# DeltaNet with a multiplicative feed-forward layer on one core: loads on one queue, clears as steps, a new order of all steps

## The chip, the core and the metric

The kernel runs on one core of a Trainium2 chip. The metric is device time in microseconds (us), the median of several runs. The core has five instruction queues: TensorE (PE, with its weight loads as PEld), VectorE (DVE), ScalarE (ACT), GpSimd (POOL) and SyncE (SP). Each works through its own queue in order and waits on semaphores where it needs a result of another. Loads and stores are issued by one of these queues and carried out by 16 DMA engines.

## The reference

Two stages follow each other. The first is a delta rule over 768 tokens for 4 batches of 8 heads of width 48; the second is a feed-forward layer over the 3072 rows of 384 values that come out of it.

```python
k_n = k / (np.linalg.norm(k, axis=-1, keepdims=True) + 1e-06)
for t in range(S):
    y[:, :, t] = einsum('bhd,bhde->bhe', q[:, :, t], state)
    v_old = einsum('bhde,bhd->bhe', state, k_n[:, :, t])
    state += beta[:, :, t] * outer(k_n[:, :, t], v[:, :, t] - v_old)
x = y.transpose(0, 2, 1, 3).reshape(3072, 384)
a, b = x @ w1, x @ w2                 # 384 x 1024 each
out = ((a * b) @ w3) @ w_out          # 1024 x 1024, 1024 x 384
```

The four weight matrices lie in memory in double precision; the kernel turns them into float32 itself.

## The kernel before

The 768 tokens are cut into 12 chunks of 64, and two chunks form a pair. Within a chunk the delta rule is solved with a triangular inverse; between chunks a state is carried on. The kernel is written as steps of many small parts, each a Python generator, and every `next` of a part issues one step's instructions. The parts, with the letter that names them in the list:

- `k`, `q`, `v`, `p` load K, Q and V; `p` loads K and then Q of a chunk in a second layout, into the buffers `perm` and `spare` (`load_perm`, L246, issues at L253). `k` and `q` use `load_crossed` (L225) and `load_tok` (L236). For chunk 0, `k` and `q` are issued on ScalarE's queue (L1205, L1216), everything else on SyncE's.
- `K`, `Q` (chunks 0 and 1) turn K and Q on TensorE (L352) and copy the result into KQ on ScalarE and VectorE (L362, L364); `d` (other chunks) does it on VectorE out of `perm` and `spare` (L339).
- `g`, `N` are the norms of K (squares on GpSimd L285, sums on VectorE L287, a square root by Newton steps, copies on ScalarE L274 and L276).
- `s` are the scores of a chunk: TensorE (L383, L389), VectorE's product (L395), and for some chunks ScalarE's copy (L407) and GpSimd's mask (L409).
- `u` and `V` are the inverse of a pair of chunks. For the first two pairs the scores are copied into `columns` (L446), transposed on VectorE (L466), the unit matrix is copied from Vb to PSUM by ScalarE (L475), and 31 pairs of VectorE operations follow (L484, L489), which are a chain of their own, with a transpose behind them (L503). Later pairs go through memory (L453, L468, L514).
- `e` is the corner, which completes a chunk's inverse: TT is filled (L549, by ScalarE and GpSimd), VectorE transposes part of it (T, L559), then two groups of products on TensorE (L576) with ScalarE's copies between (L601, L621).
- `c` is the chain from chunk to chunk (TensorE L647, VectorE L678, L687, L707, L709), `y` the outputs (TensorE L746, ScalarE L767).
- `P` is one piece of a weight matrix, 36 in all: a load on SyncE (L791) into one of five `raw` buffers, two operations on ScalarE (L799, L802), a shift on VectorE (L804) and an addition on GpSimd (L806). A buffer can be loaded again when GpSimd has added.
- `t` transposes a piece of w3 on TensorE (L841) and copies it into w3T on ScalarE (L844); `f` folds w3 and w_out into one matrix on TensorE (L855, copied at L862), in two halves for each of eight blocks.
- `a` and `b` compute a * b for the first pair's tokens (L875, L887, L891); `a`, `h`, `i`, `j` do it for later pairs with eleven products in place of more (L994, L1002, L1010, L1031, L1041). `S`, `o`, `x` multiply by the folded matrix and store (L1075, L1104, L1121 to L1166).

`ORDER`, a list of some 1,460 names, says which part takes its next step; each engine then executes its instructions in exactly that order (`in_text_order`, L168). So the list decides what is queued behind what on all five queues.

Buffers that must hold zeros are made by `padded` (L194): it allocates them and clears the whole of them, or all from a column on, on GpSimd (L198) as the program is written down, which puts all clears ahead of the list's steps: TT (2048 values a partition), perm, spare (1024 each), x_room (512), four ktok (16 each), U, T11 (8 each), late (520) and T22 (512). V0's first step, the clear of Vb (L461, L462), stands behind them.

## Time and profile before

| | |
|---|---|
| median of 3 runs | 552.52 us (552.31 to 554.47) |
| profiled execution | 554.45 us |
| its span, first to last instruction | 552.7 us |
| mean granted TensorE clock | 0.994 |
| busy: VectorE, ScalarE, GpSimd | 362.1, 187.6, 253.6 us |
| read from and written to memory by the core | 41.25 and 8.91 MB |

A row of instructions in order of time gives its start, its length, the engine and line, the operation with the tiles it writes and reads, the count, and in brackets how long the engine stood idle before it and what ended that. A row of the chain of work that ended last gives start, length and what it was. "SPq" and "ACTq" are the queues issuing a DMA. Matmuls are pipelined, so the lengths of single ones overlap; a group's length is taken from the chain, in which pieces follow each other.

### The profile page before, as it was taken

Reading aid. Unit: us, or ns where it says so; the run is one execution under the profiler, and the core shown is the slowest. Engines: PE = TensorE matmul, PEld = TensorE weight load, DVE = VectorE, ACT = ScalarE, POOL = GpSimd, SP = SyncE. Lnnn points to the kernel's source line nnn. Section 1 sums busy time; section 2 is a strip of 40 time slices with the busy share of each in tenths; the row PEclk is TensorE's granted clock in tenths of the full one; section 3 lists DMA queues with packets and bytes.
Section 4 is the critical chain, followed back from the end, with each engine's and each line's share of the span. In section 5 each row is a group of like instructions: output and inputs, shape, how many; then the busy total and the mean of one; then the engine's idle time right before and its main releaser. Section 6 shows DMA issues by size and latency. Waiting matters only on the chain.

```text
span 552.7 us, 19818 instructions
## 1 busy us (share of the span) xinstructions
PE 521.4 (94%) x8540; PEld 447.8 (81%) x8540; DVE 362.1 (66%) x814; ACT 187.6 (34%) x393; POOL 253.6 (46%) x278
## 2 busy tenths in 40 slices
PE   3686999999999999999999999999999999999997
PEld 2563666688878988889987889988899888998897
DVE  2757877798767878569967579858587654123332
ACT  4788388955633012422022430123231121300000
POOL 8466555453569960365343255510492212342141
PEclk9997999999999999999999999999999999999999
DMA  8987987669356345454553564253601220020001
GB/s 251 203 223 189 199 188 141 120 159 150 55 90 127 80 106 80 61 101 81 114 98 61 79 121 86 86 83 43 125 16 44 62 51 5 9 66 1 0 1 57
DMA packets 197687, 52.64 MB, mean 95 GB/s; under 512 B 185344, under 2 KB 191488, under 8 KB 197600
## 3 DMA queue, kind: packets, MB, share of 16 engines
q1 hardware_dynamic: 193408, 50.59, 44.6%
q10 hardware_dynamic: 4192, 0.79, 0.9%
q8 instruction: 67, 1.10, 0.8%
q14 instruction: 20, 0.16, 0.1%
HBM read 41.25 MB, written 8.91 MB: 91 GB/s over the span
## 4 chain that ended last, share of the span: by engine, by line
PE 80%; DMA 6%; ACT 5%; DVE 4%; SPq 2%; issue 1%; DVEq 0%; ACTq 0%
PE ps_f L994 33%; PE ps_f L1104 19%; PE ps_f L855 7%; PE ps_w L647 6%; PE ps_f L875 6%; PE ps_w L746 4%; PE ps_w L576 2%; DMA X<-in_q_dram 2%; PE ps_w L383 2%; PE ps_w L389 1%; DMA raw<-in_moe_w_dram 1%; DMA ktok<-in_k_dram 1%; SPq L253 1%; DVE KQ L339 1%; ACT raw L802 1%
## 5 line engine op out<-in xcount | busy, mean ns | idle before, releaser
L1002 DVE TENSOR_TENSOR ab<-ab,ps_f 128x512 f32<-128x512 f32 x80 | 54.5, 682 | 57.3 <-PE ps_f L994 56.8
L1075 POOL TENSOR_TENSOR ab<-ab 128x512 f32<-128x512 f32 (+1 forms) x56 | 61.3, 1116 | 41.8 <-PE ps_f L1104 25.4
L994 PE MATMUL ps_f<-xT,w1s 128*128 128x256 f32 x320 | 78.5, 382 | 0.0
L1041 POOL TENSOR_TENSOR ab<-ab,late 128x512 f32<-128x512 f32 x19 | 24.1, 1271 | 107.0 <-DVE ab L1002 106.3
L994 PEld LDWEIGHTS ps_f<-xT,w1s 128*128 128x128 f32 x320 | 59.9, 190 | 7.9
L1104 PE MATMUL ps_f<-w,ab 128*128 128x192 f32 x376 | 65.5, 328 | 0.0
L1104 PEld LDWEIGHTS ps_f<-w,ab 128*128 128x128 f32 x376 | 61.3, 190 | 1.3 <-issue 0.5
L409 POOL TENSOR_TENSOR PT<-PT,smask 128x512 f32<-128x512 f32 x20 | 25.5, 1277 | 54.9 <-ACT PT L407 54.9
L855 PE MATMUL ps_f<-w2s,w3T 128*128 128x384 f32 x128 | 45.9, 510 | 4.9 <-ACT w3T L844 4.9
L1104 PE MATMUL ps_f<-room,ab 128*128 128x192 f32 x272 | 47.2, 328 | 0.0
L500 DVE TENSOR_TENSOR ps_w<-ps_w,tb 128x31 f32<-128x31 f32 (+15 forms) x124 | 43.3, 349 | 4.2
L767 ACT COPY xT<-ps_w 48x256 f32<-48x256 f32 x96 | 30.4, 365 | 44.8 <-PE ps_w L746 44.3
L1104 PEld LDWEIGHTS ps_f<-room,ab 128*128 128x128 f32 x272 | 44.3, 190 | 0.6 <-issue 0.3
L495 DVE TENSOR_TENSOR tb<-ps_w,Ub 128x31 f32<-128x31 f32 (+15 forms) x124 | 41.9, 338 | 3.6 <-ACT ps_w L475 0.3
L1010 ACT COPY ab<-ps_f 128x512 f32<-128x512 f32 x20 | 11.7, 586 | 95.1 <-PE ps_f L994 95.0
L994 PE MATMUL ps_f<-xT,room 128*128 128x256 f32 x160 | 41.3, 385 | 0.3 <-DVE ab L1002 0.2
L855 PEld LDWEIGHTS ps_f<-w2s,w3T 128*128 128x128 f32 x128 | 24.4, 198 | 20.8 <-issue 6.6
L994 PE MATMUL ps_f<-xT,w2s 128*128 128x256 f32 x160 | 40.1, 381 | 0.0
L994 PE MATMUL ps_f<-x_room,w2s 128*128 128x256 f32 x160 | 38.9, 386 | 0.0
L994 PEld LDWEIGHTS ps_f<-xT,room 128*128 128x128 f32 x160 | 29.5, 190 | 5.5 <-DVE ab L1002 1.1
L994 PEld LDWEIGHTS ps_f<-x_room,w2s 128*128 128x128 f32 x160 | 29.5, 190 | 5.1 <-DVE late L1002 1.0
L994 PEld LDWEIGHTS ps_f<-xT,w2s 128*128 128x128 f32 x160 | 30.1, 190 | 4.0
(143 smaller groups left out, 977.2 us busy)
## 6 DMA issues: line engine op xcount, KB each, us to landing
raw<-in_moe_w_dram SPq DMA_DIRECT2D x16, 512.0 KB, 6.7
vtok<-in_v_dram SPq DMA_DIRECT2D x24, 192.0 KB, 4.4
raw<-in_moe_w_dram SPq DMA_DIRECT2D x24, 192.0 KB, 4.9
out_dram<-osb SPq DMA_DIRECT2D x46, 96.0 KB, 1.7
ktok<-in_k_dram SPq DMA_DIRECT2D x44, 96.0 KB, 3.4
raw<-in_moe_w_out_dram SPq DMA_DIRECT2D x8, 384.0 KB, 4.5
perm<-in_k_dram SPq DMA_DIRECT2D x40, 64.0 KB, 2.8
perm<-in_q_dram SPq DMA_DIRECT2D x32, 64.0 KB, 2.8
```

What stands on the lines that cost most here:

```text
L409: pool.tensor_tensor(out=PT, in0=PT, in1=smask[:].unsqueeze(1).to_broadcast([P, H, C]), op=ALU.mult)
L495: dve.tensor_tensor(out=tv, in0=V[:, 0 : s + 1, s : s + 1].to_broadcast([P, s + 1, n]), in1=U[:, s, s + 1 : BS].unsqueeze(1).to_broadcast( ...
L500: dve.tensor_tensor(out=o, in0=o, in1=tv, op=ALU.subtract)
L647: pe.matmul(out(ps, r, h, z), lhsT=lhs(r, h, z), rhs=rhs(r, h, z), start=True, stop=True,)
L767: act.copy(out=xT[f, p:NP:2, b : b + NR, cc, :].rearrange("p a r t -> p r a t"), in_=pyv[f, z, b : b + NR],)
L855: pe.matmul(ps[:, 0:DM], lhsT=w3Ts[jc, kc // 4][:, kc % 4 * P : kc % 4 * P + P], rhs=wo[:, kc], start=(i == 0), stop=(i == KF - 1),)
L875: pe.matmul(ps[:].rearrange("p b c t -> p b (c t)"), lhsT=w[:, m, js], rhs=x[:, m, :, c0:c1].rearrange("p b c t -> p b (c t)"), start=(m = ...
L994: pe.matmul(acc[name][:, n * i : n * i + n], lhsT=ws[b][:, P * i : P * i + P], rhs=xs[x], start=new and k == 0 and i == 0, stop=k == len(t ...
L1002: dve.tensor_tensor(out=o_, in0=x, in1=acc[name], op=ALU.add)
L1041: eng.tensor_tensor(out=Z1, in0=Z1, in1=late, op=ALU.mult)
L1075: pool.tensor_tensor(out=o_, in0=x_, in1=y_, op=op)
L1104: pe.matmul(ps[b][:, b, :], lhsT=block(u, HF * f + i, z)[:, P * b : P * b + P], rhs=ws_[w][:, i], start=first and i == 0 and (b == 0 or n ...
```

## The change

All loads are issued on SyncE's queue. `padded` no longer clears; it notes what is to be cleared and by which engine, and two new parts clear one noted region a step: `zd` (three on VectorE) and `zp` (nine on GpSimd). On VectorE only that part of TT, perm and spare is cleared which is read as zeros without being written: the first 32 of each 64 columns of TT, the upper 16 of each 32 columns of perm and spare. The list has the same steps as before and these twelve, in a new order throughout. The lines of what stands below `padded` move by 13, and by 15 from the table of parts on.

```diff
 ORDER = """
-V0 P0 k0 beta P18 P13 P0 P18 P0 P0 P11 g0 P13 K0 P18 K0 P11 P18 P10 P13 P13 q0 P3 P3 P11 g0 beta
-beta K0 K0 K0 k1 K1 P10 P11 P12 P3 P12 g0 g0 Q0 P10 g0 g0 g0 g0 g0 P8 Q0 Q0 Q0 K1 K1 K1 Q0 K1 P3
...
+V0 zp P13 beta P12 beta P13 beta P13 k0 P12 P13 P0 P0 k1 K0 t5 g0 P0 g0 g0 P12 K0 K0 K0 P11 P11 K0
+P0 zd P12 zd g0 g0 P10 P18 q0 g0 g0 K1 P10 K1 P8 g0 P10 P11 K1 t5 g0 P9 Q0 q1 K1 K1 P18 P11 P10 P8
+Q0 Q0 Q0 Q0 P3 t2 P18 P8 N0 P9 t2 N0 t3 s0 k2 t3 Q1 P5 P3 P18 P9 P2 s0 P8 zp P3 t4 t0 P3 Q1 s0 g1 zp
+s0 Q1 Q1 Q1 s1 s0 g1 zd P5 s1 P1 t0 P1 s1 P2 P1 P9 g1 s0 t1 P5 P2 s1 P5 P2 s1 p2 P4 s1 d2 g1 P6 P7
+d2 zp t4 u0 u0 s0 u1 t10 u1 P19 u0 u1 V0 V0 t1 V0 V0 P4 P6 P4 V0 P7 V0 P6 P1 V0 f1 f0 P4 P7 k3 V0
...
+    zeros = []
+
+    def padded(name, shape, n, start=0, where=None, eng=pool):
         res = []
         for i in range(n):
             t = persist.tile(shape, FP32, name=f"{name}{i}")
-            pool.memset(t[:, start:] if start else t[:], 0.0)
+            zeros.append((eng, where(t) if where else t[:, start:] if start else t[:]))
             res.append(t)
         return res

+    def zero(part):
+        for eng, t in zeros:
+            if (eng is dve) == part:
+                eng.memset(t, 0.0)
+                yield
+
-    TTx = padded("TT", [P, 2, NR, H, C], 1)[0]
+    TTx = padded("TT", [P, 2, NR, H, C], 1, where=lambda t: t[:, :, :, :, 0:BS], eng=dve)[0]
...
-    perm = padded("perm", [P, B, NP, 2, BS], 1)[0]
-    spare, x_room = (padded(x, [P, n], 1)[0] for x, n in (("spare", 1024), ("x_room", 512)))
+    perm = padded(
+        "perm", [P, B, NP, 2, BS], 1, where=lambda t: t[:, :, :, :, D - BS :], eng=dve
+    )[0]
+    spare = padded(
+        "spare", [P, 1024], 1, eng=dve,
+        where=lambda t: t[:].rearrange("p (g d) -> p g d", d=BS)[:, :, D - BS :],
+    )[0]
+    x_room = padded("x_room", [P, 512], 1)[0]
...
+    parts["zd"] = lambda: zero(True)
+    parts["zp"] = lambda: zero(False)
-        parts[f"k{m}"] = lambda m=m: load_k(m, act.dma_start if m == 0 else sync.dma_start)
+        parts[f"k{m}"] = lambda m=m: load_k(m)
-        parts[f"q{m}"] = lambda m=m: load_q(m, act.dma_start if m == 0 else sync.dma_start)
+        parts[f"q{m}"] = lambda m=m: load_q(m)
```

## The prediction

> **What bounds the kernel now.** I read the page's first part, then the busy time by stretches, then the list of who waited for whom, then the instructions of the early stretch one by one.

> ```profile
> span 552.7 us, 19818 instructions
> ...
> PE 521.4 (94%) x8540; PEld 447.8 (81%) x8540; DVE 362.1 (66%) x814; ACT 187.6 (34%) x393; POOL 253.6 (46%) x278
> ...
> 0.00:44.23 44.23, 23.72 (x490) 19.86 (x490) 22.58 (x45) 31.06 (x55) 31.32 (x46) 1.00 0.83 212
> ...
> 44.00:48.00 4.00, 2.14 (x6) 1.29 (x6) 3.58 (x14) 3.98 (x10) 2.58 (x3) 0.59 0.72 220
> 48.00:52.00 4.00, 3.81 (x8) 2.04 (x7) 3.53 (x11) 1.85 (x4) 2.24 (x2) 0.55 0.96 321
> ...
> 160.00:500.00 340.00, 337.96 (x5840) 300.23 (x5840) 231.29 (x510) 77.23 (x182) 152.68 (x164) 1.00 0.39 74
> 500.00:552.70 52.70, 48.98 (x254) 44.47 (x252) 17.46 (x28) 2.71 (x5) 12.82 (x11) 1.00 0.05 16
> ...
> PE ps_f L352 <- DMA ktok<-in_k_dram: 12.4, 4, 4.7
> PE ps_f L855 <- ACT w3T L844: 4.9, 2, 4.7
> ```

> In the rows by stretch the columns are the stretch, its length, the busy time of PE, PEld, DVE, ACT and POOL, PE's granted clock, the DMA engines' busy share and GB/s. TensorE is the bound: it stands idle 552.7 - 521.4 = 31.3 us, and 20.5 of these (44.23 - 23.72) lie before 44.23 us, another 1.9 in the next four. From 160 to 500 us it lacks 2.0 us in 340, and the tail lacks 3.7. Both kernels issue the same matmuls, so the change can gain only from the first 50 us, and can lose anywhere by making TensorE wait. In the first 50 us the list of waits names loads of K and ScalarE's copies of w3T. Behind these stands ScalarE: 31.06 us of work by 44.23, when the first inverse (V0) has its copies in PSUM and its loop on VectorE can begin. Its idle time until then is 44.23 - 31.06 = 13.2 us:

> ```profile
> 0.80 2.80 ACTq L225 DMA_DIRECT2D ktok<-in_k_dram  x4
> ...
> 3.63 1.28 ACT L799 ACT_TABLE_LOAD   x1 [3.63 <-issue]
> ...
> 8.02 0.66 ACT L799 ACTIVATE w<-raw 128x512 f32<-128x512 f32 x1 [2.10 <-DMA raw<-in_moe_w_dram]
> ...
> 11.05 0.69 ACT L799 ACTIVATE w<-raw 128x512 f32<-128x512 f32 x1 [1.78 <-DMA raw<-in_moe_w_dram]
> ...
> 15.35 0.55 ACT L799 ACTIVATE w2s<-raw 128x384 f32<-128x384 f32 x1 [1.79 <-DMA raw<-in_moe_w_out_dram]
> ...
> 20.50 0.69 ACT L799 ACTIVATE w<-raw 128x512 f32<-128x512 f32 x1 [1.82 <-DMA raw<-in_moe_w_dram]
> ...
> 43.02 1.21 ACT L475 COPY ps_w<-Vb 128x512 f32<-128x512 f32 x2
> ...
> DMA to landing us min/median/max: 3.2/5.4/7.3
> ```

> The brackets hold the idle time ahead of a row and what ended it: 3.6 us at the start, while ScalarE issues K's four loads, then 2.10 + 1.78 + 1.79 + 1.82 = 7.5 us for weight loads; 13.2 - 3.6 - 7.5 = 2.1 us are small gaps. The last row counts the weight loads of the first 60 us from issue to landing.

> V0's loop then sets when TensorE can start the first corner (L576), and the second inverse (V1) sets when it can start the corner of chunk 2:

> ```profile
> 44.44 0.19 DVE L484 TENSOR_TENSOR tb<-ps_w,Ub 128x31 f32<-128x31 f32 x1
> ...
> 48.51 14.67 PE ps_f L855 x40
> ...
> 79.92 0.71 DVE L559 STREAM_TRANSPOSE T<-TT 128x512 f32<-128x512 f32 x1 [0.91 <-ACT TT L549]
> ...
> 81.73 0.67 PE ps_w L576 x50
> ...
> 98.26 0.23 PE L389 MATMUL ps_w<-KQ 48*64 48x64 f32 x2
> ...
> 106.56 0.19 DVE L484 TENSOR_TENSOR tb<-ps_w,Ub 128x31 f32<-128x31 f32 x1
> ...
> 133.62 0.20 DVE L489 TENSOR_TENSOR ps_w<-ps_w,tb 128x31 f32<-128x31 f32 x1
> ...
> 139.35 0.71 DVE L559 STREAM_TRANSPOSE T<-TT 128x512 f32<-128x512 f32 x1 [2.95 <-POOL sq L285]
> ...
> 140.60 0.29 PE L576 MATMUL ps_w<-T,U 33*33 33x32 f32 x11
> ```

> From V0's first step to its T is 80.63 - 44.44 = 36.2 us, and TensorE comes 1.1 us later. From the scores of chunk 3 (done 98.5) to T of chunk 2 (140.06) is 41.6 us, and TensorE comes 0.5 us later. Both are all but critical.

> **The change part by part.** *Clears.* Four large ones leave the head of GpSimd's queue:

> ```profile
> 2.51 1.80 POOL L198 MEMSET TT<- 128x2048 f32 x1
> ...
> 9.32 1.02 POOL L806 TENSOR_TENSOR w2s<-w2s,raw 128x384 uint32<-128x384 uint32 x1
> ...
> 10.37 0.33 SPq L791 DMA_DIRECT2D raw<-in_moe_w_out_dram  x1
> ...
> 0.00:14.00 14.00, 4.19 (x76) 3.54 (x76) 3.76 (x5) 6.01 (x9) 12.53 (x28) 1.00 0.84 250
> 14.00:28.00 14.00, 8.70 (x215) 7.49 (x219) 9.94 (x28) 10.32 (x23) 6.97 (x8) 1.00 0.95 203
> ```

> GpSimd's first weight addition starts at 9.32, and the load that reuses its raw buffer goes out right behind it, at 10.37. With TT, perm and spare gone to VectorE and the rest behind the additions, it could start some 3 us earlier. I cost this directly at nothing, since the DMA engines are 0.84 and 0.95 busy meanwhile. VectorE gets half of TT (1024 elements a partition) and half of perm and spare (512 each). The trace has no clear on VectorE; bounds are its rows: a 128x1024 transpose 1.24 us (L466), 128x512 operations 0.4 to 0.7 (L804, L339), so 0.7 to 1.3 for TT, 1.5 to 2.7 in all. The first two stand where VectorE waits for loads anyway; spare's stands just ahead of a scores product (L395) that V0 needs and may cost up to 0.7. I take 0, near the waits it fills.

> *Loads.* K's and Q's first loads move behind weight loads on SyncE. ScalarE no longer issues K's, but its first weight piece is issued at 0.8 and lands 3.2 us later at the earliest, so of the 3.6 us idle 4.0 - 1.28 = 2.7 remain (the table load fits into the wait). The same loads stand ahead of V0 in both orders, but Q's second now goes before K's third and the second w_out piece. Of the 7.5 us I let half remain, 3.75: all of it remains if the engines' rate decides, none if the order of loads fits ScalarE's work throughout. The 2.1 us of small gaps stay.

> *Order.* Three more w3T copies now stand ahead of V0 on ScalarE:

> ```profile
> 36.95 1.56 ACT L844 COPY w3T<-ps_f 128x512 f32<-128x512 f32 x3
> ...
> 64.91 0.43 DVE L804 TENSOR_SCALAR w<-w 128x512 uint32<-128x512 uint32 x1 [1.79 <-ACT w L799]
> ...
> 70.88 0.43 DVE L804 TENSOR_SCALAR w<-w 128x512 uint32<-128x512 uint32 x1 [1.57 <-ACT w L799]
> ...
> 97.33 0.33 PE L383 MATMUL ps_w<-KQ 48*64 48x128 f32 x2 [1.26 <-ACT xT L767]
> ...
> 108.60 0.94 DVE L687 TENSOR_TENSOR X<-ps_w,wt 128x768 f32<-128x768 f32 x1
> ...
> 121.58 0.41 DVE L891 TENSOR_TENSOR ab<-ab,ps_f 128x256 f32<-128x256 f32 x1
> ...
> 165.66 1.08 PE ps_w L647 x64
> ...
> 158.06 2.79 PE ps_f L875 x12
> ```

> So V0 starts 13.2 - 1.56 - (2.7 + 3.75 + 2.1) = **3.1 us earlier**. TensorE no longer makes T wait: before, T lay ready 1.1 us; I count **1.0**. The new order puts one group of chunk 2's scores ahead of the first corner; such a group took 97.33 to 98.49, and this is work done while TensorE waits: **1.2**. V0's loop takes in two transposes (0.68 each, L339) and two reductions (0.54, L287) that stood behind it, 2.4 us; but its two longest waits for weight conversions, 1.79 and 1.57, may be filled by them. Between 2.4 lost and 3.4 gained I take **1.0 lost**.

> TensorE would then reach the first corner early. From the last wait for w3T to the corner it took 81.73 - 48.51 = 33.2 us; now it starts this stretch about 0.6 us ahead of V0's loop, at 40.7, and comes at 73 to 75, while T is ready at 80.63 - 3.1 + 1.0 = 78.5. A gap of some 4 us opens there. The trace shows what follows such a gap: behind the wait of 4.7 us the granted clock was 0.59 and 0.55, which cost 0.41 x 2.14 + 0.45 x 3.81 = 2.6 us. I take half, **1.3 lost**, as folds that wait for w3 pieces may break the gap up.

> [...]

> At the corner of chunk 2 the new order leaves TensorE less to do between chunk 3's scores and it: one product of the chain (1.08), one corner product (0.67) and three ab products (2.79 / 2 each) fewer, 5.9 us. The distance was 140.60 - 98.49 = 42.1 us, so it is 36.2 now. V1 has to fit: its loop was 27.3 us, of which I count about 2 less, since four ab products (L891, 0.41 each) and a chain product (L687, 0.94) leave it, 2.6 us, and one conversion more comes in; the 8.1 us ahead of it shrink to about 5, as the columns' copies follow the scores at once; the tail to T of 6.2 stays or loses the copies that stood in ScalarE's way (1.5). That is 35.0 to 36.5: it just fits, and I count nothing.

> Behind 160 us I count nothing: the orders are alike there, and the work between the inverses' scores and corners is as long as before or longer.

> Sum: 3.1 + 1.0 + 1.2 - 1.0 - 1.3 = 3.0 us gained. The profiled execution took 554.45 us (a span of 552.7 and 1.75 around it), so it would take 551.4; the median of the runs, 552.52, lies 1.9 below it, so I forecast **549.5 us**.

> **The rivals.** *The waits for loads stay as they are.* Then 7.5 us remain in place of 3.75 and the gain is -0.8: 553.3 us. For it: DMA shares of 0.84 and 0.95, so the engines' rate may decide; the clears never held them up. Against: the share falls to 0.83 over the 44 us, so there is slack to use.

> *V1 becomes the bound, and the kernel is slower.* If V1 needs the 41.6 us that it took before, TensorE waits 41.6 - 36.2 = 5.4 us at chunk 2's corner and pays the clock once more, 2.6: the 3.0 become -5.0, 557.5 us. It ends slower than before once V1 needs over 39.2. For it: no slack was left there before (0.5 us). Against: part of those 41.6 us was ScalarE's ab copies in front of TT's.

> *The order fits throughout.* No waits for loads remain, 3.75 more: 545.8 us. For it: ScalarE is idle only 2.1 us outside these waits. Against: the first pieces cannot land sooner.

> That the change does not do what it says is no rival of its own: the clears leave GpSimd's head for certain, and if they were not on the path, that is the first rival.

> **How the numbers follow.** My forecast, 547.5 to 551.5: 0.40. Waits stay (551.5 to 555.5): 0.24. V1 binds: 0.18. All fits: 0.18. About 0.5%, 2.8 us, is what a measurement of this kernel can tell from no change, so faster means below 549.7: 0.18 and somewhat over half of 0.40 (0.26) give 0.44; slower means above 555.3: 0.18 and a tail of 0.04 give 0.22; within it 0.34. The range reaches from the case in which all fits to most of the case of V1: 545 to 557.

> **What would show it.** Right: ScalarE's rows of V0's copies (L488 in the changed kernel) end near 41 us, its idle time ahead of weight conversions halves, and TensorE shows a wait of some us before the first corner (L589) with a lower granted clock behind it. Wrong: V0 starts no earlier than 44 us (loads decide); a wait at chunk 2's corner (V1); more than 3 us of idle TensorE between 160 and 500 us, which would mean that the new order loses where I counted nothing.

## The result and the profile after the change

| | before | changed |
|---|---|---|
| median, us | 552.84 (552.31 to 554.47, 4 runs) | 571.78 (565.52 to 573.47, 4 runs) |
| ratio, with its 95% interval | | 1.0317 (1.0235 to 1.0399) |
| profiled execution; its span | 554.45; 552.7 | 570.98; 569.3 |
| mean granted TensorE clock, profiled | 0.994 | 0.976 |

The ratio is that of the means, and times are those of the faster of two states, so that one run of one version (the filled gap, 576.68 us) is left out. The changed kernel is 3.2% slower, 19 us by the medians; I had forecast 3 us less. The same kernel, run again later beside two variants, gave 572.45 us and a ratio of 1.0321 (1.0281 to 1.0362).

The page of the changed kernel, first its busy times and then, of the DMA queues, the one that carries instructions (packets, megabytes, share of the engines):

```profile
span 569.3 us, 19829 instructions
...
PE 529.8 (93%) x8540; PEld 453.7 (80%) x8540; DVE 368.8 (65%) x817; ACT 187.8 (33%) x393; POOL 250.0 (44%) x275
...
q8 instruction: 67, 1.10, 0.8%
```

Of the 16.6 us in the span, 8.4 are longer busy TensorE (529.8 against 521.4) and 8.2 idle TensorE (39.5 against 31.3). The matmuls are the same 8540, and the records of the clock give 13.7 us lost to it against 3.4 (0.024 of 569.3, 0.006 of 552.7), so the longer busy time is a lower clock in the main. The rows by stretch, to be held against those of before:

```profile
0.00:46.05 46.05, 30.42 (x504) 24.31 (x505) 22.50 (x49) 32.89 (x59) 26.73 (x38) 0.85 0.87 222
...
84.00:98.00 14.00, 11.30 (x367) 8.21 (x363) 9.29 (x15) 7.28 (x13) 8.36 (x10) 0.74 0.69 136
...
160.00:500.00 340.00, 332.09 (x5935) 294.03 (x5934) 233.78 (x523) 78.80 (x185) 145.53 (x155) 0.99 0.38 71
500.00:569.30 69.30, 65.51 (x342) 59.57 (x340) 22.73 (x37) 3.30 (x6) 17.41 (x17) 1.00 0.09 28
```

From 160 to 500 us TensorE now lacks 7.9 us in 340, where it lacked 2.0. The list of waits says for what:

```profile
PE ps_w L660 <- issue: 4.4, 4, 2.3
PE ps_w L589 <- DVE T L572: 4.1, 2, 3.3
...
PE ps_w L589 <- issue: 2.7, 2, 2.0
PE ps_f L365 <- DMA ktok<-in_k_dram: 2.7, 3, 1.7
...
PE ps_w L396 <- ACT PT L420: 1.8, 1, 1.8
```

Waits for K have shrunk from 12.4 to 2.7 us, though the first wait, 5.8 us, is now one for beta, whose products come first. What is new are waits put down to "issue", which means that no semaphore held the instruction: 8.6 us in all with 1.5 in smaller groups, against 0.8 before, where this is the largest group:

```profile
PE ps_w L746 <- issue: 0.5, 1, 0.5
```

Now the rows in order of time. First ScalarE up to the first inverse (V0), and VectorE's first step of its loop:

```profile
4.97 0.66 ACT L812 ACTIVATE w<-raw 128x512 f32<-128x512 f32 x1 [2.89 <-DMA raw<-in_moe_w_dram]
...
12.04 0.56 ACT L812 ACTIVATE w2s<-raw 128x384 f32<-128x384 f32 x1 [2.39 <-DMA raw<-in_moe_w_out_dram]
...
15.06 0.58 ACT L375 COPY KQ<-ps_f 48x512 f32<-48x512 f32 x1 [2.00 <-DVE KQ L377]
...
45.42 0.60 ACT L488 COPY ps_w<-Vb 128x512 f32<-128x512 f32 x1
...
46.05 0.19 DVE L497 TENSOR_TENSOR tb<-ps_w,Ub 128x31 f32<-128x31 f32 x1 [0.40 <-ACT ps_w L488]
```

V0's loop starts at 46.05 us, 1.6 later than before. Then the end of V0 and the first corner, and two places further on, at 156 and 382 us:

```profile
75.90 1.25 DVE L516 STREAM_TRANSPOSE Ub<-ps_w 128x1024 f32<-128x1024 f32 x1
...
77.25 0.19 DVE L314 SCALAR_TENSOR_TENSOR nt<-ss,seed 128x32 f32<-128x32 f32 x1
77.28 2.10 POOL L562 COPY TT<-Ub 32x512 f32<-32x512 f32 x2 [0.53 <-DVE seed L307]
77.47 0.95 DVE L317 TENSOR_TENSOR nt<-nt,seed 128x32 f32<-128x32 f32 x1
78.45 0.98 DVE L319 SCALAR_TENSOR_TENSOR nr<-nt,seed 128x32 f32<-128x32 f32 x1
...
82.44 0.70 DVE L572 STREAM_TRANSPOSE T<-TT 128x512 f32<-128x512 f32 x1
...
83.20 1.13 PE L589 MATMUL ps_w<-T,U 33*33 33x32 f32 x64 [3.33 <-DVE T L572]
84.26 5.13 PE L868 MATMUL ps_f<-w2s,w3T 128*128 128x384 f32 x8
...
155.41 0.96 PE L660 MATMUL ps_w<-X,ktok 64*64 64x48 f32 x51
158.67 0.39 PE L660 MATMUL ps_w<-X,ktok 64*64 64x48 f32 x13 [2.31 <-issue]
...
382.53 1.31 POOL L1088 TENSOR_TENSOR ab<-ab 128x512 f32<-128x512 f32 x1
...
382.75 1.15 DVE L314 SCALAR_TENSOR_TENSOR nt<-ss,seed 128x32 f32<-128x32 f32 x1
383.93 0.75 DVE L317 TENSOR_TENSOR nt<-nt,seed 128x32 f32<-128x32 f32 x1
...
389.01 0.33 PE L396 MATMUL ps_w<-KQ 48*64 48x128 f32 x2 [1.80 <-ACT PT L420]
```

Four things are to be seen. The norms of chunks 2 and 3 (N1, 77.07 to 82.5) stand ahead of T, which begins as soon as they end. TensorE waits 3.33 us for T, and the eight fold products behind it take 5.13 us where before such eight took 2.85 (the row below). At 156 us TensorE stops 2.31 us in the middle of a group of 64 products, with nothing to wait for. At 389 us it waits for a copy of PT, which stands behind another run of norms. A group of folds before:

```profile
89.28 2.85 PE L855 MATMUL ps_f<-w2s,w3T 128*128 128x384 f32 x8
```

To say where the time goes I give each product the mean time that its kind takes in the kernel before, outside recorded half clock (0.33 us for one of a fold, 0.22 for an a * b product, 0.01 to 0.04 for the small ones), and add these times up in the order in which TensorE issues the products. Both kernels issue the same products, so the same sum is the same amount of work done, at whatever clock; the total is 518.4 us in each. The table gives the time at which each kernel starts the product that reaches the sum; the third and fifth column are experiments told below. With the changed kernel's own mean times the differences between the two kernels move by 0.4 us at most.

| work done, us | before | old list in the changed kernel | changed | three places mended |
|---|---|---|---|---|
| 55 | 82.1 | 84.4 | 79.1 | 77.4 |
| 80 | 109.2 | 111.9 | 115.7 | 114.5 |
| 110 | 139.0 | 141.5 | 145.1 | 144.2 |
| 125 | 155.3 | 158.6 | 163.5 | 161.2 |
| 335 | 367.2 | 370.9 | 377.4 | 374.7 |
| 350 | 382.4 | 386.1 | 395.9 | 393.5 |
| 425 | 456.3 | 460.0 | 471.5 | 469.1 |
| 455 | 486.7 | 490.3 | 503.4 | 500.4 |
| last product | 548.7 | 552.3 | 565.2 | 562.2 |

V0 ends at the same time in both (75.90 against 75.68 us), and with a work of 55 done the changed kernel is 3.0 us ahead. Up to a work of 80 it then takes 36.6 us against 27.1: 9.5 lost. From 80 to 110 the two are alike. From 110 to the last product it takes 420.1 us against 409.7: 10.4 lost. The stretch from 55 to 80, before and changed:

```profile
82.10:109.20 27.10, 25.21 (x786) 18.71 (x774) 19.21 (x45) 23.64 (x43) 14.89 (x14) 1.00 0.68 130
```

```profile
79.10:115.70 36.60, 29.66 (x928) 22.13 (x919) 23.01 (x48) 27.92 (x53) 18.35 (x20) 0.86 0.58 121
```

TensorE is idle for 6.9 us of it in place of 1.9, and the clock takes 0.14 of 36.6 us, 5.1 us, where it took nothing.

### The profile page after: what moved, and what is told of

It is laid out like the page before. It is cut to its first block, busy times and chain, and to the rows that moved or that the text cites. A ratio compares the mean times of both kernels' runs of the same rounds, so it can differ in the third digit from the quotient of the medians.

```text
span 569.3 us, 19829 instructions
## 1 busy us (share of the span) xinstructions
PE 529.8 (93%) x8540; PEld 453.7 (80%) x8540; DVE 368.8 (65%) x817; ACT 187.8 (33%) x393; POOL 250.0 (44%) x275
## 4 chain that ended last, share of the span: by engine, by line
PE 74%; DVE 8%; DMA 4%; issue 3%; ACT 1%; SPq 1%; DVEq 0%; ACTq 0%
PE ps_f L1007 31%; PE ps_f L1117 17%; PE ps_f L888 8%; PE ps_w L660 5%; PE ps_w L759 4%; PE ps_w L589 3%; PE ps_f L868 3%; PE ps_w L396 2%; PE ps_w L402 1%; DVE ps_w L502 1%; DVE tb L497 1%; DVE tb L508 1%; DVE ps_w L513 1%; DMA Ub<-Ud 1%; DMA perm<-in_k_dram 1%
## 5 line engine op out<-in xcount | busy, mean ns | idle before, releaser
L1007 PE MATMUL ps_f<-xT,w1s 128*128 128x256 f32 x320 | 78.5, 383 | 0.0
L1117 PEld LDWEIGHTS ps_f<-room,ab 128*128 128x128 f32 x272 | 44.4, 190 | 1.0 <-POOL xT L993 0.7
```

The lines of the kernel that those rows point to most:

```text
L1007: pe.matmul(acc[name][:, n * i : n * i + n], lhsT=ws[b][:, P * i : P * i + P], rhs=xs[x], start=new and k == 0 and i == 0, stop=k == len(t ...
L1117: pe.matmul(ps[b][:, b, :], lhsT=block(u, HF * f + i, z)[:, P * b : P * b + P], rhs=ws_[w][:, i], start=first and i == 0 and (b == 0 or n ...
```

## The experiments

The theory after the result: the new list costs, not the queue and not the clears; it costs in several places, by putting work in front of what TensorE needs and by crowding small products. The rivals: queue or clears cost; or it is only a clock that differs from run to run (0.964 to 0.991 in the four runs).

### Old list in the changed kernel; new list in the kernel before

The first keeps loads and clears as changed and takes the old list behind them, the second does the reverse.

```diff
 ORDER = """
-V0 zp P13 beta P12 beta P13 beta P13 k0 P12 P13 P0 P0 k1 K0 t5 g0 P0 g0 g0 P12 K0 K0 K0 P11 P11 K0
+V0 zd zd zd zp zp zp zp zp zp zp zp zp P0 k0 beta P18 P13 P0 P18 P0 P0 P11 g0 P13 K0 P18 K0 P11 P18
...
```

> The list of before in the changed kernel: V0's clear of Vb first, then the twelve clears as steps, then the old list; all loads on SyncE, half of the clearing by VectorE. Theory A (the new list costs the 19 us, queue and clears cost nothing): 551 to 555 us, first corner near 81.7 us, granted clock 0.99. Rival B (loads of chunk 0 behind SyncE's queue, or the clears by VectorE, are the cost): 566 to 573 us. Rival C (the clock differs from run to run and the kernels are alike): runs of both kinds, between 552 and 573.

Measured: 558.09 us, ratio 1.0066 (1.0033 to 1.0099), by the ratio 3.7 us more than before: 3 us above what Theory A allowed and far below Rival B.

> The list of the changed kernel without its clears, in the kernel before: K and Q of chunk 0 issued by ScalarE, all clears at the head of GpSimd's queue. Theory A (the list): 567 to 574 us. Rival B (queue and clears): 551 to 555 us. If list, queue and clears only hurt together, the time lies between, 555 to 566 us.

Measured: 580.58 us, ratio 1.0475 (1.0429 to 1.0521). The list costs, and more so without the other edits (1.0475, above every time that I expected) than with them (1.0317). In this trace V0's loop starts only at 52.2 us, which fits a list made for loads that SyncE issues; which of its steps needs them I did not test. Loads and clears cost a little by themselves under the old list.

### Clears alone, loads alone

```diff
-        parts[f"k{m}"] = lambda m=m: load_k(m)
+        parts[f"k{m}"] = lambda m=m: load_k(m, act.dma_start if m == 0 else sync.dma_start)
...
-        parts[f"q{m}"] = lambda m=m: load_q(m)
+        parts[f"q{m}"] = lambda m=m: load_q(m, act.dma_start if m == 0 else sync.dma_start)
```

This, made in the old list in the changed kernel, leaves the clears alone. The reverse edit in the kernel before gives the loads alone.

> The old list with the clears as steps at its head (three on VectorE), K and Q of chunk 0 issued by ScalarE as before: the clears alone. My prediction cost them at 0: 552 to 555 us. Rival (the clears on VectorE stand ahead of what the loads feed, or their writes hold up the loads): 556 to 560 us, as with clears and loads together (558.1).

Measured: 554.96 us, ratio 1.0003 (0.9984 to 1.0022): nothing.

> The kernel before with K and Q of chunk 0 issued on SyncE's queue, clears at the head of GpSimd's queue: the loads alone. If the loads of K, which now stand behind the first weight load on SyncE, are what cost 3.7 us in the old list: TensorE's waits for K of 15 us in place of 12.4, V0's loop near 47 us in place of 44.4, 555 to 559 us. Rival (ScalarE, free of issuing for 2.8 us, starts sooner and V0 with it): 549 to 552 us.

Measured: 557.70 us, ratio 1.0043 (1.0018 to 1.0067), 2.4 us (1.0 to 3.7). TensorE's waits in these two, clears alone first, then loads alone:

```profile
PE ps_f L365 <- DMA ktok<-in_k_dram: 10.8, 3, 4.5
```

```profile
PE ps_f L352 <- DMA ktok<-in_k_dram: 17.3, 5, 10.2
```

K behind SyncE's queue comes later in the old list (17.3 us of waits against 12.4 before); the three clears on VectorE take 0.91, 0.48 and 0.48 us and are off the path.

### Where in the list: joints

Four kernels take the one list up to a step and the other's remaining steps behind it, all in the changed kernel: old to the last step of the second inverse, then new; old to the first step of the fourth inverse, then new; new to the first step of the third inverse, then old; new to the first outputs, then old. A fifth, new to the last step of the second inverse and old behind it, has no time, since its order deadlocks. The edit of the first of them, against the old list:

```diff
 b4 V1 V1 P35 V1 V1
-g2 c1 e2 e2 e2 e2
+a06 b6 a06 b6 a00 v3 n3 c1 e2 e2
...
```

> The changed kernel with the old list (clears at its head) up to the last step of the second inverse, then the remaining steps in the new list's order. Theory A by the landmarks: 561 to 566 us, that is 8 to 12 us lost behind 150 us. If the loss is all early: 551 to 555 us.

Measured: 572.87 us, ratio 1.0356 (1.0310 to 1.0402), 7 us above what I expected.

> The changed kernel with the old list (clears at its head) up to the first step of the fourth inverse (about 230 us), then the remaining steps in the new list's order. The old list throughout took 558.1 us, the new one behind the second inverse 572.9. The traces put 5 to 6 us of the loss behind 240 us (the wait of 1.8 us at 389, stalls of 2.2 us at 469 and 487, the clock behind them): 562 to 565 us. If each place at which two orders are joined costs several us by itself: 566 to 575 us.

Measured: 564.38 us, ratio 1.0208 (1.0169 to 1.0246): the new list behind 230 us alone adds 6.3 us to 558.1 (7.9 by the ratios, 1.0208 against 1.0066). This trace has the same 2.0 us wait for PT and stalls put down to "issue" of 1.0, 0.8 and 0.6 us.

> The changed kernel with the new list up to its first step of the third inverse (about 150 us in its trace, the second corner of the first pair begun), then the remaining steps in the old list's order. The old list in the changed kernel took 558.1 us, the new list behind the second inverse added 14.8 us to it. Theory A (most of the loss is made by the late part of the new list): 554 to 561 us. Rival (early and late part each cost about the same and only one of the two shows): 566 to 572 us.

Measured: 569.75 us, ratio 1.0254 (1.0201 to 1.0307): the rival's number, though its reason isn't shown. Right behind the joint stand waits that neither list has:

```profile
PE ps_w L660 <- ACT late L614: 4.1, 1, 4.1
PE ps_w L759 <- DVE X L700: 2.2, 1, 2.2
```

> The changed kernel with the new list up to the outputs of the first pair of chunks (about 110 us), then the old list's order: a joint further forward than the one at 150 us, which gave 569.8 us with two waits of 2.2 and 4.1 us right behind the joint. If the early part of the new list costs what the work done by 110 us shows (some 3 us against the old list in the changed kernel, 558.1): 559 to 563 us. If the early part costs 10 us, whatever the joint: 567 to 571 us.

Measured: 573.28 us, ratio 1.0339 (1.0292 to 1.0385), above both of the times expected, again with waits of its own behind the joint:

```profile
PE ps_w L660 <- ACT xT L780: 5.5, 1, 5.5
PE ps_f L888 <- ACT w L875: 2.5, 1, 2.5
```

So joints say that the late part costs (twice, in stretches far from the joint, with the same wait for PT of 2.0 and 1.8 us), but not how much the early part does: a joint breaks the order that it should leave alone. What the early part costs I take from the work done only: from 55 to 80 the changed kernel takes 36.6 us and, run again, 38.0, the old list in it 27.5.

### The norms behind T

```diff
-e0 t14 e1 t12 N1 s2 e0 P21 P21 P29 e0 f6 P24 P26 e0 t14 s2 P23 P23 e1
+e0 t14 e1 t12 s2 e0 P21 P21 P29 e0 f6 P24 P26 e0 t14 N1 s2 P23 P23 e1
```

> One step moved in the changed kernel: the norms of chunks 2 and 3 (15 operations on VectorE, 5.4 us) go from ahead of the first corner's T to behind it. Theory A (the norms make T late, TensorE idles 3.3 us and then runs at half clock): T near 80.5, idle time ahead of the first corner 1 to 2 us, clock of 84 to 98 us above 0.9, 3 to 6 us gained, 566 to 569 us. Rival (the copies into TT by ScalarE and GpSimd end last anyway): T moves by under 0.5 us and the time stays within 2 us of 571.8.

Measured: 571.27 us, ratio 1.0292 (1.0239 to 1.0346). T and the corner as expected, and a stall behind them:

```profile
80.62 0.71 DVE L572 STREAM_TRANSPOSE T<-TT 128x512 f32<-128x512 f32 x1 [3.17 <-POOL tb L602]
...
81.38 0.76 PE L589 MATMUL ps_w<-T,U 33*33 33x32 f32 x64 [1.39 <-DVE seed L307]
...
96.12 0.27 PE L589 MATMUL ps_w<-tb,late 64*33 64x32 f32 x2 [2.45 <-issue]
```

T came 1.8 us sooner and the wait shrank from 3.33 to 1.39, but the time did not fall by anything that can be measured: the stall at 96 us took 2.45 in place of 1.96, and others came ahead of it (0.96 at 91 us, and 0.57 and 0.59 for VectorE's PT, which now stands behind the norms).

### The gap filled

```diff
-        for x in range(4):
+        for x in list(range(4)) * (4 if (jc, hf) == (7, 0) else 1):
             pe.transpose(ps[:, x, :], w3[:, x * P : (x + 1) * P], ident[:])
```

> The changed kernel with one transposition of a w3 piece (4 products, 8 records, 1.05 us) issued four times in place of once, just ahead of the score products that precede the first corner, so that TensorE works through most of the 3.3 us in which it waits for T (the same values are written again). Theory (the wait costs nothing itself, since the second inverse's loop bounds this stretch, but the clock behind it does): wait under 0.7 us, clock of 84 to 98 us at 0.95 or more in place of 0.74, 3 to 4 us gained, 567 to 569 us. Rival (the clock falls for another reason, the fetch stall of 2 us at 95): clock of 84 to 98 below 0.9, time 570 to 573 us.

Measured: 569.65 us, ratio 1.0275 (1.0217 to 1.0332), not to be told from the changed kernel's 1.0317. I had the filling wrong: the sixteen products took 1.91 us, not over 4, so the wait only fell to 2.57 us, and the stall at 96 us was 2.97; the clock of 84 to 98 us was 0.78. Whether the clock behind the gap costs by itself stays open.

### Large products moved into the crowds

Seven steps of large products, each moved forward a few places (three of the five spots are shown).

```diff
-e1 P24 c0 P21 c0 e1 y0 P26 P26 d3 P24 P27 v1 n1 e1 y0 P28 f7 c0 s3
+e1 P24 c0 P21 c0 f7 e1 y0 P26 P26 d3 P24 P27 v1 n1 e1 y0 P28 c0 s3
...
-c2 g2 P35 y2 c2 b1 g2 g2 g2 d5 y2 b4 T T d5 c2 b4 a07 a07 a01
+c2 g2 P35 y2 b4 a07 c2 b1 g2 g2 g2 d5 y2 T T d5 c2 b4 a07 a01
...
-i43 n11 c10 e11 e11 e11 c10 h43 c11 c11 i43 i43 h43 h43 y10 c11 oD4 oA4 y10 c11 xA4 y11
+i43 n11 c10 e11 h43 e11 e11 c10 c11 c11 i43 i43 h43 h43 oD4 y10 c11 oA4 y10 c11 xA4 y11
```

> Seven steps of large products moved a few places forward in the changed kernel, each into a stretch of several hundred small products at which TensorE stalls with nothing to wait for (96, 159, 231, 469, 487 us; 7.2 us in all). The stalls lie a multiple of about 127 products apart, and the profile counts 67 packets of 16 KB on a queue for instructions. Theory F (TensorE works through a block of instructions faster than the next one is fetched): these stalls fall from 8.5 to under 3 us, and the time by 5 to 8 us, 564 to 567 us. Rival (an unseen dependency): stalls of the same length stand at the same steps or move with them, time within 2 us of 571.8.

Measured: 581.96 us, ratio 1.0465 (1.0405 to 1.0525), 10 us slower than the changed kernel where I expected 5 to 8 less. The stalls put down to "issue" fell only from 8.6 to 6.5 us, and new waits came in, for T (6.4 us in all) and for GpSimd's product (3.1).

> Both edits together, the norms behind T and the seven steps spread. If both causes hold and are independent, 8 to 13 us are gained, 559 to 564 us. If neither holds, 570 to 573 us.

Measured: 579.72 us, ratio 1.0412 (1.0339 to 1.0485). A miss too. The stall at 159 us is gone and that at 487 too, but where a step came too early TensorE waits for its input, as here at 489 us (both edits together), where a step of the last layer is ahead of GpSimd's product:

```profile
489.33 2.90 PE L1117 MATMUL ps_f<-room,ab 128*128 128x192 f32 x8 [3.15 <-POOL ab L1054]
```

### What a stall is: a run of small products without any wait

One group of 48 score products of chunk 4 in the kernel before is issued 16 times over.

```diff
-            for h in range(H):
+            for h in list(range(H)) * (16 if m == 4 and r == 0 else 1):
```

> The kernel before, in which one group of 48 score products of chunk 4 (at about 155 us) is issued 16 times over, so that 720 more small products follow each other without any wait for data (they write the same values again). At the 18 to 20 ns a product that such groups show it would add 13 to 14 us. Theory F: the group runs in pieces of about 127 products with stalls between, so that a piece takes 3.5 to 4.5 us, 20 to 25 us in all: 573 to 578 us. Rival (no limit of supply): one unbroken run, 566 to 568 us.

Measured: 581.13 us in one run, 28 us above before, in place of 13 to 14. The 768 products take 22.5 us (154.5 to 177.0) where 48 took 1.1, so 21.4 of the 28 us lie in them; behind them stand new stalls of 0.5 to 1.3 us. No data are waited for, and yet:

```profile
163.00:167.00 4.00, 4.00 (x123) 4.00 (x119) 0.00 (x0) 0.00 (x0) 0.00 (x0) 0.50 0.02 4
168.00:172.00 4.00, 4.00 (x214) 4.00 (x206) 0.00 (x0) 0.00 (x0) 0.00 (x0) 1.00 0.02 4
```

```profile
172.97 0.28 PE L389 MATMUL ps_w<-KQ 48*64 48x64 f32 x2 [0.68 <-issue]
...
176.43 0.32 PE L383 MATMUL ps_w<-KQ 48*64 48x128 f32 x1 [0.63 <-issue]
```

Counted through the trace, exactly 128 products lie between the two stalls, and they take 3.46 us with the stall, 2.83 without. At half clock (163 to 167 us) TensorE does 123 in 4 us and never stalls; at full clock it did 214 in 4 us and then stalled. The queue of instructions moved 67 packets, 1.10 MB, in the changed kernel: 16.4 KB each. A product is two instructions (8540 products and as many weight loads), so 128 products are 256 instructions, and 17,080 in 67 packets are 255 each. In the changed kernel the stalls at 154 and 159 us lie 127 products apart, those at 231 and 240 us 254. So I take it that instructions arrive in blocks of 256, an estimate from these counts, and a new block for every 3.5 us or so is what this run got.

The packets of that queue, which the trace has one by one, show the cause directly. In this run they start at 156.24, 159.85, 163.40, 167.10, 170.60 and 174.09 us, and the three stalls within the repeated products, of 1.77, 0.68 and 0.63 us (at 158.6, 173.0 and 176.4 us), end 1.41, 1.25 and 1.41 us after one of them has landed. In all 20 traces of this document no two of these packets start less than 3.2 us apart, and each of the 97 stalls over 0.4 us that is put down to "issue" ends 1.2 to 2.0 us after a packet has landed. Their place is set by the count of products and not by the step that stands there: in the twelve traces with the new list at 96 us the stall stands after 980 or 981 products, before a product of the corner, of the chain or, where a fold was moved ahead, of the fold. So the rival that they are unseen waits for data is out.

### Large products taken out of the kernel before

```diff
-c2 e2 P34 e2 b6 P35 P35 e2 c2 c2 e3 a03 g2 g2 P33 b6 y2 g2 P33 g2 d5 d5 p5 c2 c2 y2 a04 e3 s4 N2
+c2 e2 P34 e2 P35 P35 e2 c2 c2 e3 g2 g2 P33 y2 g2 P33 g2 d5 d5 p5 c2 c2 y2 e3 s4 b6 b6 a03 a04 N2
```

> The kernel before, with three steps of large products (b6, a03, a04; 18 products, 4.3 us) taken out of the stretch of small ones at 142 to 156 us and put behind it, so that some 540 small products follow each other. Theory F (instructions are fetched in blocks of about 127 products, and a run of small products uses up a block faster than the next arrives): stalls without a releaser, 127 products or a multiple apart, 2 to 5 us in all, where the kernel before has none over 0.2; 556 to 560 us. Rival (the stalls have to do with the new list's other steps, or are waits on data): idle time there is put down to named releasers or is absent.

Measured: 559.06 us, ratio 1.0119 (1.0092 to 1.0145). The waits between 142 and 157 us:

```profile
PE ps_w L574 <- ACT xT L765: 1.8, 1, 1.8
PE ps_w L645 <- ACT TT L619: 1.0, 2, 0.7
PE ps_w L744 <- DVE X L685: 0.6, 1, 0.6
PE ps_w L744 <- issue: 0.5, 1, 0.5
```

The size was as expected and the cause was not: here the large products had covered the copies and products of other engines between the steps of the chain, and only 0.5 us of stall came in. Crowding small products costs in two ways, and which one shows depends on the spot.

### Three places mended

The norms behind T as above, b4 and a07 ahead of c2 as above, and the sums and norms of chunks 10 and 11 a few steps forward:

```diff
-a31 j32 a31 a31 a31 h32 e8 a31 e8 h32 g5 g5 g5 g5 g5 h32 h31 e8 s10 e8 i31 g5 N5 s10 p11 i32
+a31 j32 a31 a31 g5 g5 g5 g5 a31 h32 e8 a31 e8 g5 h32 g5 N5 h32 h31 e8 s10 e8 i31 s10 p11 i32
```

> Three places of the changed kernel mended by moving a few steps: the norms of chunks 2 and 3 go behind the first corner's T; two steps of large products go ahead of the last product of chunk 2's chain, where TensorE stalled 2.3 us at 159 us; the sums and norms of chunks 10 and 11 go a few steps forward, since their 15 operations (5.0 us at 382 us, beside GpSimd's products, 3.5 us elsewhere) end just ahead of the score product for which TensorE waits 1.8 us at 389 us. If these waits cost what the trace shows, idle time and clock behind them: 1 to 3, 2 and 3 us, together 6 to 8, 564 to 566 us. Rival (the time lost shows up at the next wait instead): 569 to 573 us.

Measured: 567.89 us, ratio 1.0268 (1.0238 to 1.0297). Then once more on one chip with the changed kernel, and without the early one of the three:

> The changed kernel once more, beside the two versions below on one chip, as their base: 566 to 574 us (its four runs so far: 565.5 to 573.5).

> The three mended places once more. In its trace it was 3.2 us ahead of the changed kernel in the work behind 110 us, and 3 to 4 us ahead of it at 110 us, of which 2.9 us lie in a lower clock between 28 and 42 us that differs from run to run. Theory (all three places count): 5 to 7 us faster than the changed kernel on this chip. Rival (only the two late places count): 2.5 to 4 us faster. If the medians so far differ by luck: within 1.5 us.

> Only the two late places mended, the products ahead of the last product of chunk 2's chain (159 us) and the sums and norms of chunks 10 and 11 (382 us); the norms of chunks 2 and 3 stay ahead of T. Theory: by the traces 3.2 us faster than the changed kernel, 2 to 4.5 us with what differs from run to run, and the three places beat it by 1 to 3 us more. Rival (moving the norms behind T gives nothing, as the one run of it alone suggested, 571.3 against 571.8): the same as the three places within 1 us.

Measured: changed 572.45 us, ratio 1.0321 (1.0281 to 1.0362); three places 568.15, 1.0254 (1.0221 to 1.0287); the two late ones alone 568.70, 1.0274 (1.0234 to 1.0315). The medians fall by 4.3 and 3.8 us; the first interval only just touches that of the changed kernel, the second overlaps it by half, so this is good to 2 or 3 us. The rival fits on the early place: the norms ahead of T cost about 0.5 us by both pairs of medians (571.8 and 571.3, 568.7 and 568.2), which these runs can't tell from nothing, though the list of waits shows 3.3 there. Behind a work of 110 the mended kernel takes 562.2 - 144.2 = 418.0 us, the two late places alone 417.9, the changed kernel 420.1 and, run again, 421.6, and the kernel before 409.7: two small moves give back a fifth to a third of the late loss. Most of it comes from the first: from 110 to 125 the versions with it take 16.1 to 17.0 us against 18.4 and 19.5. From 335 to 350 they take 17.3 to 18.8 against 18.5 and 18.6, since a wait of 1.2 us for a product (L1044, at 383 to 384 us) has come in where 1.8 for PT has gone.

## Why the prediction was wrong, point by point

**"V0 starts 3.1 us earlier": it started 1.6 later** (46.05; 43.7 to 46.5 in the new list's other traces in the changed kernel). The saving on loads came in part: 11.1 us of waits (3.6 + 7.5) became 2.89 + 2.24 + 2.39 + 0.33 = 7.9, where I had 6.5. What failed is "the 2.1 us of small gaps stay": a copy now stands behind VectorE's (2.00), others behind scores (1.29) and norms (0.66), so that ScalarE is idle for 13.2 us as before; and it has 32.89 us of work by 46.05 in place of 31.06. The clock does not explain it. Where the trace has no record of the clock the rows count it as 1.00, and the first record stands at 34.5 us before and at 24.0 in the changed kernel; ahead of it the products that transpose w3 follow each other at 213 ns, as at a recorded half clock, in place of 109. So both kernels seem to have run at half clock for most of this stretch: to 34.5 us before, to 24.0 and from 27.5 to 41.1 in the changed kernel. In the trace of the new list joined at 150 us the half clock ended at 31.1, and V0 started at 46.15 all the same.

**"TensorE no longer makes T wait", T at 78.5: T came at 82.44.** V0's loop was shorter (46.05 to 75.90, 29.9 us against 31.2), where I had it 1.0 longer, but I did not count N1, which the list had moved ahead of T: 15 operations, 5.4 us. By the mended versions this step was wrong and nearly free, as far as the runs can tell: the next waits and stalls took it back.

**"1.2 for a group of scores", "1.3 for the clock".** Here lies the first of the two steps that failed. The gap was there as forecast, 3.33 us, with the clock at half behind it, and 0.74 over 84 to 98 us. But from a work of 55 to one of 80 the kernel lost 9.5 us, where my four terms from 1.0 to -1.3 come to nothing: TensorE is idle for 5.0 us more, where I had counted on a gain of 2.2, and the clock takes 5.1, where I had 1.3. The clock goes to half twice, at 82.1 and at 95.7 us, each time behind 3.4 us in which TensorE was busy for only 1.2 and 1.7: the first holds most of the wait for T, the second most of the stall of 1.96 us at an instruction block's end, which I did not foresee. Both lists issue four groups of eight folds about there, but before they start at 83.3, 89.3, 99.3 and 104.1 us, and now at 84.3 and 99.4, 108.9 and 114.0, with some 370 small products between the first two. What the wait, the stall or the clock is worth by itself stays open: the two edits there, the norms and the filled gap, gave nothing in time that can be told from zero.

**"V1 just fits": right.** V1 took 35.6 us from chunk 3's scores (done at 107.3) to T (142.85), within my 35.0 to 36.5, and chunk 2's corner, at 143.6, had no wait for T; of the two in the list of waits one is the first corner and the other at 221 us (0.8).

**"Behind 160 us I count nothing, the orders are alike there": this is the second step that failed, and the one that cost most.** From a work of 110 on (145 us, 139 before) 10.4 us are lost, 8.3 of them behind 163 us. Idle TensorE in it is 10.8 us against 3.1, and the clock takes 1.7. Of the idle time 6.2 are stalls at the end of an instruction block (0.5 before), 1.8 the wait for PT, 0.8 for T. I had compared the order of the large parts, not how many small products follow each other, and I did not look at the norms, which now run beside work of GpSimd: 15 operations took 3.5 to 3.6 us in all six places before, and 3.5 to 5.5 in the changed kernel, single ones 0.4 to 1.2 us in place of 0.19. Moved behind T, with no operation of GpSimd beside them, those of chunks 2 and 3 took 3.5 in place of 5.4.

In the rows at 77 and 382 us three of VectorE's operations on two inputs took 0.95, 0.98 and 1.15 us beside GpSimd's two copies of 1.05 us on average and its product of 1.31, and VectorE's operation on one input at 382.53 us kept 0.18 beside that product.

**"Clears cost 0": right** under the old list (1.0003). **Loads "gain half of the waits"**: under the old list they cost 2.4 us; under the new one, loads and clears together gain (571.78 against 580.58 us without them), and the waits for K fall to 2.7 us, but the corner still waits for V0 and N1 (3.33 us).

In sum, loads and clears cost 3.7 us under the old list (1.8 to 5.5), and the new list in place of the old adds 13.7 (571.78 against 558.09). Shown by runs are that the list costs, that its part behind 230 us costs 6 to 8, what the loads cost, and that a stall is a fetch of instructions; the three places together are clear of the noise (some 4 us), the two late ones alone barely. That the stalls as a whole are worth what they last, and where the early 9.5 us go, is only read from the traces. A part is the clock, which differs from run to run: the four runs of the changed kernel went from 565.5 us at 0.991 to 573.5 at 0.964. It isn't all: of all runs of the kernel before the slowest took 559.9 us, at 0.997.

None of the versions tried beats the kernel before.

## What to carry to other kernels

An order made by hand is a balance of every stretch, so a new one has to be priced in all of them, above all where nothing seems to move: count, for each stretch, the small products between two large ones and what the list puts in front of the operation that TensorE waits for next. An engine that runs ahead of the chain which bounds the stretch need not gain: here 3.0 us of lead were lost at the next corner. The same number of large products covers a stretch or not by where they stand in it. A wait in the profile is not what removing it gives: here 1.9 of 3.3 us of wait were worth about 0.5, within the noise, a stall of 2.3 us about its size, and a wait of 1.8 us little.
